# Seven tokens per row at the start, weights cast by DMA in one burst, and the inversion and the casts moved in a fused attention and feed-forward kernel

## The chip, the cores and the metric

The kernel runs on one core of one Trainium2 chip. The time is device time in microseconds (us) of the whole program. Executions of one kernel mostly agree within a few tenths of a per cent to one per cent. Each run has a state: "slow" when it is over 1.5% above the fastest run of the same kernel, at a lower granted clock. Ratios below use fast runs only: a ratio is the mean time of one kernel's fast runs over the mean of the other's fast runs of the same rounds, so it is not quite the ratio of the medians that stand beside it.

Engines: PE is TensorE, ACT is ScalarE, DVE is VectorE, POOL is GpSimd, SP is SyncE, and SPq is the DMA queue that SyncE feeds.

## The reference

```python
# q, k, v: (8 batches, 12 heads, 448 tokens, 64); cap = 30
scores = cap * tanh((q @ k.T) / sqrt(64) / cap)
attn   = softmax(scores)                  # exp, divided by its sum over the keys
x      = attn @ v                         # -> (3584 tokens, 768)
out    = maximum(x @ w1, x @ w2) @ w_out  # w1, w2: 768x1024, w_out: 1024x768
```

## The kernel before

A pair is two heads (48 pairs), a group is three pairs (16 groups). The engine streams are scheduled by hand: the order of the Python calls is the order on each engine. The feed-forward matmuls of earlier batches are dealt out as filler between the attention steps (`F(n)` issues n of them). It uses max(a, b) = relu(a - b) + b, so w1 - w2 is made once by VectorE (`subtract`), and w2 is turned by PE so that w2 times w_out can be made once too.

The first four groups have q and k (cast to bf16 in `kqf`) transposed by PE; from group 4 on one DMA transpose (`cross`) does it, into `qkT`. A group then goes this way: evict three pairs from PSUM to `u` (two buffers), gather the softmax sums (`sums`), invert them (`rec_s`), send the reciprocals to DRAM (`rec_d`) and back as a broadcast (`rec_b`), multiply `u` by them into `xT`.

```python
    def transposes(i):                      # groups 0 to 3, one pair
        g, n = divmod(i, L)
        ps = mm_psum.tile([P, 512], f32, name="mm").bitcast(bf16)
        for j in range(8):
            nc.tensor.transpose(ps[:, j * P : (j + 1) * P], kqf[g % 2][:, n, j, :], ident)
        nc.vector.tensor_copy(qkT_of(g)[:, n, :, :].rearrange("p j c -> p (j c)"), ps)

    def invert(g, n0=0, n1=G):
        ...
        nc.vector.reciprocal(t[:m, :], sums[g, n0][:m, :])
        nc.sync.dma_start(out=d[:m, :], in_=t[:m, :])             # rec_d, in DRAM
        for h in range(2):
            nc.sync.dma_start(out=rb[64 * h : 64 * h + 64, ...],  # rec_b, two DMAs
                              in_=flat[h : h + 1, :, :].to_broadcast([64, n1 - n0, S]))

    # end of moe(b): one 128x768 output tile, token 3p + j in partition p
    rows = out[b0 * S : b0 * S + NJ * P, :].rearrange("(p j) n -> p j n", j=NJ)
    nc.sync.dma_start(out=rows[:, j, :], in_=osb)

    for i in range(N):                       # one pair after another
        ...                                  # matmuls with v, evict to u, gather, filler
        if i + 1 < N:
            qk(i + 1, 3); ex(i + 1, 4, 7)
        for f, a in todo[i]:                 # loads, casts on POOL, DMA transposes
            f(*a)
        F(6)
        if i + 2 < NT * L:
            transposes(i + 2)
        F(6)
        if i == N - 1:
            invert(g, 0, G - 1)
        elif i >= G and n == 0:
            invert(g - 1)
        if i >= G and n == 1:
            normalize(g - 1)                 # six multiplies on POOL, releases u
        ...
```

Of the kernel before, what the change touches and what calls it, by code (L numbers as in the profile page):

```python
# [10 lines left out]
def kernel(  # L11
# [11 lines left out]
    nc = tc.nc  # L23
# [13 lines left out]
    L = 3  # L37
    G = 3
    Q0 = 4 * P
    NJ = 3  # L40
    scale = 1.0 / (D ** 0.5)

    ctx.enter_context(tc.manual_schedule())
# [24 lines left out]
    kf = [t[:, :, 0:4, :] for t in kqf]  # L68
    qf = [t[:, :, 4:8, :] for t in kqf]

    ident = const.tile([P, P], bf16, name="ident")
    make_identity(nc, ident)

# [14 lines left out]
    def half(b):  # L88
        return slice(0, 64) if b % 2 == 0 else slice(64, P)

    def load(g, what, n0=0, n1=L):
        b, p = divmod(g * L, NP)
        h0, h1 = 2 * (p + n0), 2 * (p + n1)
        src = {"k": k, "q": q, "v": v}[what]
        if (g, what) not in raw:
            raw[g, what] = (
                stage.tile([P, 2 * L, NJ * D], f32, name=what + "m"),
                stage.tile([P, 2 * L if what == "q" else L, D], f32, name=what + "l"),
            )
        m, l = raw[g, what]  # L100
        nc.sync.dma_start(  # L101
            out=m[:, 2 * n0 : 2 * n1, :],
            in_=src[b, h0:h1, 0 : NJ * P, :].rearrange("h (p j) d -> p h (j d)", j=NJ),
        )
        if what == "q":
            nc.sync.dma_start(
                out=l[half(b), 2 * n0 : 2 * n1, :],
                in_=src[b, h0:h1, NJ * P : S, :].rearrange("h p d -> p h d"),
            )
        else:  # L110
            for par in range(2):
                nc.sync.dma_start(  # L112
                    out=l[64 * par : 64 * par + 64, n0:n1, :],
                    in_=src[b, h0 + par : h1 : 2, NJ * P : S, :].rearrange("h p d -> p h d"),
                )

    def cast(eng, g, what, n0=0, n1=L):

        b = g * L // NP
        m, l = raw[g, what]  # L120
        if what == "v":
            for par in range(2):
                r = slice(64 * par, 64 * par + 64)
                eng.tensor_copy(  # L124
                    vp[g % 2][:, n0:n1, par, :, r],
                    m[:, 2 * n0 + par : 2 * n1 : 2, :].rearrange("p n (j d) -> p n j d", d=D),
                )
                eng.tensor_copy(vl[g % 2][r, n0:n1, r], l[r, n0:n1, :])
            return
        o = b % 2 if what == "q" else 0  # L130
        t = (kf if what == "k" else qf)[g % 2]
        eng.tensor_copy(  # L132
            t[:, n0:n1, o : o + NJ, :].rearrange("p n j (h d) -> p n h j d", h=2),
            m[:, 2 * n0 : 2 * n1, :].rearrange("p (n h) (j d) -> p n h j d", h=2, d=D),
        )
        if what == "q":
            eng.tensor_copy(
                t[half(b), n0:n1, 3 * (1 - o), :],
                l[half(b), 2 * n0 : 2 * n1, :].rearrange("p (n h) d -> p n (h d)", h=2),
            )  # L140
        else:
            for par in range(2):
                r = slice(64 * par, 64 * par + 64)
                eng.tensor_copy(t[r, n0:n1, 3, r], l[r, n0:n1, :])
# [11 lines left out]
    def load_wo(f):  # L156
        nc.gpsimd.dma_start(
            out=wo_sb[:, f : f + 2, :], in_=moe_w_out[f * P : (f + 2) * P, :].rearrange("(c p) n -> p c n", p=P)
        )
# [39 lines left out]
    def qkT_of(g):  # L199
        if g not in qkT:  # L200
            qkT[g] = stage.tile([P, L, 8, P], bf16, name="qkT")
        return qkT[g]

    def transposes(i):

        g, n = divmod(i, L)
        ps = mm_psum.tile([P, 512], f32, name="mm").bitcast(bf16)
        for j in range(8):
            nc.tensor.transpose(ps[:, j * P : (j + 1) * P], kqf[g % 2][:, n, j, :], ident)  # L209
        nc.vector.tensor_copy(qkT_of(g)[:, n, :, :].rearrange("p j c -> p (j c)"), ps)  # L210

    def cross(g):

# [4 lines left out]
    def qk(i, j):  # L218

        g, n = divmod(i, L)  # L220
        t = qkT[g][:, n, :, :].rearrange("p j c -> p (j c)")
        o = Q0 + 64 * (i // NP % 2)
        qTn = t[:, o : o + S]
        if j == 0:
            tanh[i] = att.tile([P, 7, S], bf16, name="tanh", bufs=1)
            expo[i] = att.tile([P, 7, S], bf16, name="expo")
        s = s_psum.tile([P, 2, 512], f32, name="s")
        if j < NJ:
            for h in range(2):
                r = slice(64 * h, 64 * h + 64)  # L230
                nc.tensor.matmul(s[:, h, :S], t[r, j * P : (j + 1) * P], qTn[r, :])  # L231
            nc.scalar.activation(tanh[i][:, 2 * j : 2 * j + 2, :], s[:, :, :S], AF.Tanh, scale=scale / cap)  # L232
        else:
            nc.tensor.matmul(s[:, 0, :S], t[:, 3 * P : 4 * P], qTn)  # L234
            nc.scalar.activation(tanh[i][:, 6, :], s[:, 0, :S], AF.Tanh, scale=scale / cap)  # L235

    def ex(i, c0, c1):
        nc.scalar.activation(expo[i][:, c0:c1, :], tanh[i][:, c0:c1, :], AF.Exp, scale=float(cap))  # L238
# [71 lines left out]
    def moe(b):  # L310
# [12 lines left out]
        for t in range(3) if b % 2 == 0 else range(3, 7):  # L323
            osb = opool.tile([P, DM], f32, name="osb")
            ts = slice(t * P, (t + 1) * P)
            for half in range(2):
                hs = slice(half * (DM // 2), (half + 1) * (DM // 2))
                ps = mm_psum.tile([P, 512], f32, name="mm")
                for c in range(KC):
                    nc.tensor.matmul(ps[:, : DM // 2], x[:, c, ts], wm_sb[:, c, hs], start=(c == 0), stop=False)  # L330
                    yield
                for f in range(FC):
                    nc.tensor.matmul(  # L333
                        ps[:, : DM // 2], g[:, f, ts], wo_sb[:, f, hs], start=False, stop=(f == FC - 1)
                    )
                    yield
                nc.vector.tensor_copy(osb[:, hs], ps[:, : DM // 2])  # L337
            if t == 3:
                for n in range(2):
                    r0 = (b - 1 + n) * S + NJ * P  # L340
                    nc.sync.dma_start(out=out[r0 : r0 + 64, :], in_=osb[64 * n : 64 * n + 64, :])
            else:
                b0, j = (b, t) if t < 3 else (b, t - 4)
                rows = out[b0 * S : b0 * S + NJ * P, :].rearrange("(p j) n -> p j n", j=NJ)
                nc.sync.dma_start(out=rows[:, j, :], in_=osb)

    fill_q = []

# [7 lines left out]


    NL = N // L
    NT = 4
    todo = [[] for _ in range(N)]  # L360

    def at(i, f, *a):
        todo[i].append((f, a))

    for g in range(2, NL):
        e = 0 if g < NT else 2
        at(3 * g - 6 - e, load, g, "k")
        at(3 * g - 5 - e, load, g, "q")
        at(3 * g - 4, load, g, "v")
        at(3 * g - (5 if e else 4), cast, nc.gpsimd, g, "k")  # L370
        at(3 * g - (5 if e else 3), cast, nc.gpsimd, g, "q")
        at(3 * g - 2, cast, nc.gpsimd, g, "v")
        if g >= NT:
            at(3 * g - 4, cross, g)
    at(1, cast, nc.gpsimd, 1, "v")
    at(0, load_wo, 6)
    for c in range(KC):
        at(1 + c, load_w2, c)
        at(2 + c, load_w1, c)
    MS = 3  # L380

    fill_const(nc.vector, 0)
    fill_const(nc.gpsimd, 1)
    load_wo(0)
    for n0, n1 in ((0, 1), (1, L)):
        for what in "kqv":
            load(0, what, n0, n1)
    for what in "kqv":
        load(1, what)
    for what in "kq":  # L390
        cast(nc.vector, 0, what, 0, 1)
    transposes(0)
    cast(nc.vector, 0, "v", 0, 1)
    for what in "kqv":
        cast(nc.vector, 0, what, 1, L)
    qk(0, 0)
    qk(0, 1)
    ex(0, 0, 4)
    qk(0, 2)
    qk(0, 3)  # L400
    ex(0, 4, 7)
    cast(nc.gpsimd, 1, "k")
    load_wo(2)
    cast(nc.gpsimd, 1, "q")
    load_wo(4)
    transposes(1)
    qk(1, 0)
    qk(1, 1)

    for i in range(N):  # L410
# [22 lines left out]
        if hp == 3 and b > 1:  # L433
            fill_q.append(moe(b - 1))
        F(4 if late else 8)
        if i + 1 < N:
            qk(i + 1, 3)
            ex(i + 1, 4, 7)
        for f, a in todo[i]:
            f(*a)  # L440
        F(6)
        if i + 2 < NT * L:
            transposes(i + 2)
        F(6)
        if i == N - 1:
            invert(g, 0, G - 1)
        elif i >= G and n == 0:
            invert(g - 1)
        if i >= G and n == 1:
            normalize(g - 1)  # L450
        if i + 2 < N:
            qk(i + 2, 0)
            qk(i + 2, 1)
# [7 lines left out]
    normalize(N // G - 1, G - 1, G, nc.vector)  # L461
    fill_q.append(moe(B - 1))
    F(10 ** 9)

# [1 line left out]
_INS = ['q', 'k', 'v', 'cap', 'moe_w1', 'moe_w2', 'moe_w_out']  # L466
_OUTS = [((3584, 768), 'float32')]
# [30 lines left out]
```

## Time and profile before

| | before |
|---|---|
| time, median of 3 runs | 391.78 us (391.11 to 392.51) |
| span of the profiled run | 390.3 us |
| PE busy | 358.5 us (92%), full after some 80 us |
| PE busy in the first 80 us | 57.91 us |
| end of the last normalization with a DMA transpose ahead of it (group 13) | 325.4 us |
| one group in the steady part | 20.2 us |

The busy line and the slices say which engine is full and when; the list of waits says who waits for whom; a timeline of one engine gives the order in which a queue that never overtakes works off its list. The prediction shows and reads these lines.

### The profile page before, as it was taken

The page shows a single profiled execution, that of the slowest core. Times are in us where ns is not written, and L with a number is a line of the kernel's source. Part 1 is how long each engine was busy: PE and PEld are TensorE (multiplying, and loading weights), DVE is VectorE, ACT ScalarE, POOL GpSimd, SP SyncE. Part 2 cuts the span into 40 slices and gives each one's busy share as a digit, 9 for nine tenths or more (in the row PEclk, how much of TensorE's full clock was granted, in tenths as well). Part 3 has the DMA queues.
Part 4 walks back from the last instruction along what each step waited for, and adds up shares of the span by engine and source line. Part 5 has one row for each costly group of instructions (what it writes and reads, how often), then busy time and mean ns, then how long its engine had stood idle before and what let it go on. Part 6 is the DMA issues. An engine that isn't in the chain of part 4 may idle for free.

```text
span 390.3 us, 5720 instructions
## 1 busy us (share of the span) xinstructions
PE 358.5 (92%) x2128; PEld 171.8 (44%) x2128; DVE 164.3 (42%) x248; ACT 292.4 (75%) x289; POOL 199.6 (51%) x254
## 2 busy tenths in 40 slices
PE   3468896999999999989998999999999999999995
PEld 1123443544444444434443445444444444455563
DVE  5332657774434533253325433352345333633421
ACT  2699995878899799978998899889998899400000
POOL 4272269674638374656657464729482733651000
PEclk9995998999999999999999999999999999999999
DMA  6998899786779768967989597969796751322022
GB/s 142 280 252 180 242 288 274 198 202 165 149 199 252 198 171 199 260 181 192 217 225 223 142 237 210 255 166 225 219 188 179 166 142 65 90 73 100 23 81 81
DMA packets 106596, 71.50 MB, mean 183 GB/s; under 512 B 61384, under 2 KB 99400, under 8 KB 106568
## 3 DMA queue, kind: packets, MB, share of 16 engines
q1 hardware_dynamic: 104616, 67.99, 67.6%
q0 software_dynamic: 1952, 3.15, 4.6%
q8 instruction: 16, 0.26, 0.3%
q14 instruction: 12, 0.10, 0.1%
HBM read 53.48 MB, written 11.18 MB: 166 GB/s over the span
## 4 chain that ended last, share of the span: by engine, by line
PE 54%; DMA 17%; ACT 7%; SPq 6%; POOL 6%; DVE 5%; issue 3%; POOLq 0%; DVEq 0%; ACTq 0%
PE mm L318 15%; PE mm L333 11%; PE mm L330 9%; PE pv L250 8%; DMA rec_d<-rec_s 7%; DMA rec_b<-rec_d 6%; POOL xT L305 6%; PE s L231 5%; ACT expo L238 3%; ACT tanh L232 3%; DMA vm<-in_v_dram 3%; PE pv L259 2%; SPq L112 2%; SPq L101 1%; DMA xT<-in_moe_w_dram 1%
## 5 line engine op out<-in xcount | busy, mean ns | idle before, releaser
L232 ACT ACTIVATE tanh<-s 128x896 bf16<-128x896 f32 x144 | 126.0, 909 | 36.2 <-PE s L231 35.9
L305 POOL TENSOR_TENSOR xT<-u,rec_b 64x448 bf16<-64x448 f32 x95 | 108.2, 1139 | 86.1 <-DMA rec_b<-rec_d 73.8
L238 ACT ACTIVATE expo<-tanh 128x1792 bf16<-128x1792 bf16 x96 | 144.9, 1510 | 3.0
L265 DVE COPY u<-pv 128x896 f32<-128x896 f32 x48 | 52.3, 1091 | 105.3 <-PE pv L259 80.6
L333 PE MATMUL mm<-wo_sb,gT 128*128 128x384 bf16 x448 | 88.8, 327 | 0.0
L318 PE MATMUL mm<-xT,wd_sb 128*128 128x448 bf16 x384 | 80.8, 353 | 3.3 <-POOL xT L305 1.7
L330 PE MATMUL mm<-wm_sb,xT 128*128 128x384 bf16 x336 | 68.0, 327 | 1.8 <-DVE osb L337 1.8
L250 PE MATMUL pv<-expo,vp 128*128 128x448 bf16 x288 | 66.3, 367 | 1.1 <-ACT expo L238 1.1
L333 PEld LDWEIGHTS <-gT 128*128 128x128 bf16 x448 | 41.9, 98 | 36.5 <-issue 10.8
L337 DVE COPY osb<-mm 128x384 f32<-128x384 f32 x56 | 31.0, 555 | 59.9 <-PE mm L333 54.9
L318 PEld LDWEIGHTS <-wd_sb 128*128 128x128 bf16 x384 | 35.4, 98 | 43.9 <-issue 14.5
L231 PE MATMUL s<-qkT 64*128 64x448 bf16 x288 | 46.0, 370 | 7.7 <-DVE qkT L210 5.2
L322 DVE TENSOR_SCALAR gT<-mm 128x448 bf16<-128x448 f32 x64 | 39.9, 623 | 29.6 <-PE mm L318 28.6
L330 PEld LDWEIGHTS <-xT 128*128 128x128 bf16 x336 | 31.7, 98 | 28.6 <-issue 8.7
L250 PEld LDWEIGHTS <-vp 128*128 128x128 bf16 x288 | 28.2, 101 | 29.1 <-issue 7.7
L132 POOL CAST kqf<-qm 128x1152 bf16<-128x1152 f32 x15 | 17.2, 1147 | 33.9 <-DMA qm<-in_q_dram 33.7
L235 ACT ACTIVATE tanh<-s 128x448 bf16<-128x448 f32 x48 | 26.0, 542 | 4.3 <-PE s L234 4.1
L124 POOL CAST vp<-vm 128x576 bf16<-128x576 f32 x30 | 19.9, 665 | 14.2 <-DMA vm<-in_v_dram 9.4
L132 POOL CAST kqf<-km 128x1152 bf16<-128x1152 f32 x15 | 17.2, 1147 | 12.7 <-DMA km<-in_k_dram 11.9
L231 PEld LDWEIGHTS <-qkT 64*128 64x128 bf16 x288 | 10.9, 96 | 22.8 <-issue 15.1
L209 PE MATMUL mm<-ident,kqf 128*128 128x128 bf16 x96 | 9.8, 248 | 11.5 <-DVE kqf L132 7.7
L186 PE MATMUL mm<-wo_sb,w2T 128*128 128x384 bf16 x96 | 18.7, 328 | 0.0
(44 smaller groups left out, 158.9 us busy)
## 6 DMA issues: line engine op xcount, KB each, us to landing
rec_b<-rec_d SPq DMA_DIRECT2D x30, 336.0 KB, 5.0
out_dram<-osb SPq DMA_DIRECT2D x24, 384.0 KB, 3.9
km<-in_k_dram SPq DMA_DIRECT2D x15, 576.0 KB, 7.0
qm<-in_q_dram SPq DMA_DIRECT2D x15, 576.0 KB, 4.5
vm<-in_v_dram SPq DMA_DIRECT2D x15, 576.0 KB, 4.4
xT<-in_moe_w_dram SPq DMA_DIRECT2D x6, 512.0 KB
wo_sb<-in_moe_w_out_dram POOLq DMA_DIRECT2D x4, 384.0 KB, 7.3
gT<-in_moe_w_dram POOLq DMA_DIRECT2D x6, 256.0 KB, 5.8
```

The lines of the kernel that those rows point to most:

```text
L132: eng.tensor_copy(t[:, n0:n1, o : o + NJ, :].rearrange("p n j (h d) -> p n h j d", h=2), m[:, 2 * n0 : 2 * n1, :].rearrange("p (n h) (j d) ...
L231: nc.tensor.matmul(s[:, h, :S], t[r, j * P : (j + 1) * P], qTn[r, :])
L232: nc.scalar.activation(tanh[i][:, 2 * j : 2 * j + 2, :], s[:, :, :S], AF.Tanh, scale=scale / cap)
L238: nc.scalar.activation(expo[i][:, c0:c1, :], tanh[i][:, c0:c1, :], AF.Exp, scale=float(cap))
L250: nc.tensor.matmul(ps[:, h, :S], vp[g % 2][:, n, h, j, :], e[:, 2 * j + h, :], start=(j == 0), stop=False)
L265: nc.vector.tensor_copy(U[g][:, :, n, :], pvt[i][:, :, :S])
L305: eng.tensor_mul(xT[b // 2][r, hp, cs], U[g][r, h, n, :], rec[g, n0][r, n - n0, :])
L318: nc.tensor.matmul(ps[:, :S], wd_sb[:, c, f * P : (f + 1) * P], x[:, c, cs], start=(c == 0), stop=(c == KC - 1))
L322: nc.vector.tensor_relu(g[:, f, cs], ps[:, :S])
L330: nc.tensor.matmul(ps[:, : DM // 2], x[:, c, ts], wm_sb[:, c, hs], start=(c == 0), stop=False)
L333: nc.tensor.matmul(ps[:, : DM // 2], g[:, f, ts], wo_sb[:, f, hs], start=False, stop=(f == FC - 1))
L337: nc.vector.tensor_copy(osb[:, hs], ps[:, : DM // 2])
```

## The change

Its intent: the start should need fewer and longer DMA rows, the weights should arrive early, and the normalization of a group should be done sooner, so that its buffer comes free sooner. Four parts:

1. In the first four groups a partition holds seven consecutive tokens of a head (1792-byte rows), and one DMA loads k or q where two or three did. The transposes become 26 of 64x64 and one of 128x128 per pair. The output rows of the first two batches are then ordered by seven too, and their stores are written in another form.
2. w_out and w2 are cast by DMAs that POOL issues back to back near the start. The w1 loads stay where they were.
3. The cast of v moves to the front of its iteration's list, one iteration earlier.
4. `invert` moves ahead of the list of loads and casts (`todo`), and so does `normalize`.

```diff
+            for a in range(2):                     # transposes(i), 26 of them
+                r = slice(64 * a, 64 * a + 64)
+                nc.tensor.transpose(ps[r, to : to + 64], x[r, c : c + D], ident[r, r])
+        nc.tensor.transpose(ps[:, NJ * P : Q0], x[:, NJ * P : Q0], ident)
 ...
-                rows = out[b0 * S : b0 * S + NJ * P, :].rearrange("(p j) n -> p j n", j=NJ)
-                nc.sync.dma_start(out=rows[:, j, :], in_=osb)
+                if wide:                           # batches 2 to 7: the same store as before
+                    nc.sync.dma_start(out=o[: NJ * P, :].rearrange("(p j) n -> p j n", j=NJ)[:, j, :], in_=osb)
+                else:                              # batches 0 and 1: six stores
+                    o = o.rearrange("(r j) n -> j r n", j=R7)
+                    nc.sync.dma_start(out=o[2 * j : 2 * j + 2, :, :], in_=osb)
 ...
         for g >= 4:  # iteration of each load; k, q, v
-            3g - 8, 3g - 7, 3g - 4
+            3g - 9, 3g - 8, 3g - 7
 ...
+        if i == N - 1:
+            invert(g, 0, G - 1)
+        elif i >= G and n == 0:
+            invert(g - 1)
         if i + 1 < N:
             qk(i + 1, 3)
             ex(i + 1, 4, 7)
+        if i >= G and n == 1:
+            normalize(g - 1)
         for f, a in todo[i]:
             f(*a)
         F(6)
         if i + 2 < NT * L:
             transposes(i + 2)
         F(6)
-        if i == N - 1:
-            invert(g, 0, G - 1)
-        elif i >= G and n == 0:
-            invert(g - 1)
-        if i >= G and n == 1:
-            normalize(g - 1)
```

(The load times are condensed to two lines here; the loads, the casts and the start are cut.)

More of the change, by code (lines that the diff above doesn't have):

```diff
@@ L40 @@
     NJ = 3
+    NT = 4
+    R7 = S // 64
     scale = 1.0 / (D ** 0.5)
@@ L69, with flat @@
     qf = [t[:, :, 4:8, :] for t in kqf]
+    def flat(g):
+        return kqf[g % 2].rearrange("p n j c -> p n (j c)")
     ident = const.tile([P, P], bf16, name="ident")
@@ L89, in half, with rows, raw_of @@
         return slice(0, 64) if b % 2 == 0 else slice(64, P)
+    def rows(t, b, h0, h1):
+        return t[b, h0:h1, :, :].rearrange("h (r j) d -> (h r) (j d)", j=R7)
+    def raw_of(g, what):
+        if (g, what) not in raw:
+            raw[g, what] = stage.tile([P, 2 * L * NJ * D + (2 * L if what == "q" else L) * D], f32, name=what + "r")
+        t = raw[g, what]
+        m = t[:, : 2 * L * NJ * D].rearrange("p (h c) -> p h c", c=NJ * D)
+        l = t[:, 2 * L * NJ * D :].rearrange("p (h d) -> p h d", d=D)
+        return t, m, l
     def load(g, what, n0=0, n1=L):
@@ L94, in load @@
         src = {"k": k, "q": q, "v": v}[what]
-        if (g, what) not in raw:
-            raw[g, what] = (
-                stage.tile([P, 2 * L, NJ * D], f32, name=what + "m"),
-                stage.tile([P, 2 * L if what == "q" else L, D], f32, name=what + "l"),
+        t, m, l = raw_of(g, what)
+        if g < NT and what == "v":
+            x = rows(src, b, h0, h1).rearrange("(h r) c -> r h c", r=64)
+            for a in range(2):
+                nc.sync.dma_start(
+                    out=m[64 * a : 64 * a + 64, 2 * n0 : 2 * n1, :], in_=x[:, :, NJ * D * a : NJ * D * (a + 1)]
+                )
+            for par in range(2):
+                nc.sync.dma_start(
+                    out=l[64 * par : 64 * par + 64, n0:n1, :], in_=x[:, par::2, 2 * NJ * D :]
+                )
+            return
+        if g < NT:
+            nc.sync.dma_start(
+                out=t[:, n0 * S : n1 * S].rearrange("p (n c) -> p n c", c=S),
+                in_=rows(src, b, h0, h1).rearrange("(n p) c -> p n c", p=P),
             )
-        m, l = raw[g, what]
+            return
         nc.sync.dma_start(
@@ L119, in cast @@
         b = g * L // NP
-        m, l = raw[g, what]
+        x, m, l = raw_of(g, what)
         if what == "v":
@@ L128, in cast @@
                 eng.tensor_copy(vl[g % 2][r, n0:n1, r], l[r, n0:n1, :])
+            return
+        if g < NT:
+            x = x[:, n0 * S : n1 * S].rearrange("p (n c) -> p n c", c=S)
+            if what == "q":
+                eng.tensor_copy(flat(g)[:, n0:n1, Q0 : Q0 + S], x)
+                return
+            eng.tensor_copy(flat(g)[:, n0:n1, : NJ * P], x[:, :, : NJ * P])
+            for par in range(2):
+                r = slice(64 * par, 64 * par + 64)
+                eng.tensor_copy(kf[g % 2][r, n0:n1, 3, r], x[r, :, NJ * P :])
             return
@@ L207, in transposes @@
         ps = mm_psum.tile([P, 512], f32, name="mm").bitcast(bf16)
-        for j in range(8):
-            nc.tensor.transpose(ps[:, j * P : (j + 1) * P], kqf[g % 2][:, n, j, :], ident)
-        nc.vector.tensor_copy(qkT_of(g)[:, n, :, :].rearrange("p j c -> p (j c)"), ps)
+        x = flat(g)[:, n, :]
+        todo = [(j * D, (j % 3) * P + (j // 3) * 64) for j in range(6)]
+        odd = i // NP % 2
+        todo += [(Q0 + j * D, Q0 + (64 * j if not odd else 0 if j == 6 else 64 + 64 * j)) for j in range(R7)]
+        for c, to in todo:
+            for a in range(2):
+                r = slice(64 * a, 64 * a + 64)
+                nc.tensor.transpose(ps[r, to : to + 64], x[r, c : c + D], ident[r, r])
+        nc.tensor.transpose(ps[:, NJ * P : Q0], x[:, NJ * P : Q0], ident)
+        nc.vector.tensor_copy(qkT_of(g)[:, n, :, :].rearrange("p j c -> p (j c)")[:, : Q0 + S], ps[:, : Q0 + S])
     def cross(g):
@@ L221, in qk @@
         t = qkT[g][:, n, :, :].rearrange("p j c -> p (j c)")
-        o = Q0 + 64 * (i // NP % 2)
+        o = Q0 + (64 * (i // NP % 2) if g >= NT else 0)
         qTn = t[:, o : o + S]
@@ L337, in moe @@
                 nc.vector.tensor_copy(osb[:, hs], ps[:, : DM // 2])
+            wide = b * NP >= NT * L
             if t == 3:
                 for n in range(2):
-                    r0 = (b - 1 + n) * S + NJ * P
-                    nc.sync.dma_start(out=out[r0 : r0 + 64, :], in_=osb[64 * n : 64 * n + 64, :])
-            else:
-                b0, j = (b, t) if t < 3 else (b, t - 4)
-                rows = out[b0 * S : b0 * S + NJ * P, :].rearrange("(p j) n -> p j n", j=NJ)
-                nc.sync.dma_start(out=rows[:, j, :], in_=osb)
+                    o = out[(b - 1 + n) * S : (b + n) * S, :]
+                    to = o[NJ * P : S, :] if wide else o.rearrange("(r j) n -> r j n", j=R7)[:, R7 - 1, :]
+                    nc.sync.dma_start(out=to, in_=osb[64 * n : 64 * n + 64, :])
+            else:
+                j = t if t < 3 else t - 4
+                o = out[b * S : (b + 1) * S, :]
+                if wide:
[3 more added lines that the diff above has]
+                    nc.sync.dma_start(out=o[2 * j : 2 * j + 2, :, :], in_=osb)
     fill_q = []
@@ L358 @@
     NL = N // L
-    NT = 4
     todo = [[] for _ in range(N)]
@@ L365 @@
     for g in range(2, NL):
-        e = 0 if g < NT else 2
-        at(3 * g - 6 - e, load, g, "k")
-        at(3 * g - 5 - e, load, g, "q")
-        at(3 * g - 4, load, g, "v")
-        at(3 * g - (5 if e else 4), cast, nc.gpsimd, g, "k")
-        at(3 * g - (5 if e else 3), cast, nc.gpsimd, g, "q")
-        at(3 * g - 2, cast, nc.gpsimd, g, "v")
-        if g >= NT:
+        if g < NT:
+            for what, e in (("k", 6), ("q", 6), ("v", 5)):
+                at(3 * g - e, load, g, what)
+            e = 0
+            at(3 * g - 5, cast, nc.gpsimd, g, "k")
+            at(3 * g - 4, cast, nc.gpsimd, g, "q")
+        else:
+            at(3 * g - 9, load, g, "k")
+            at(3 * g - 8, load, g, "q")
+            at(3 * g - 5, cast, nc.gpsimd, g, "k")
+            at(3 * g - 5, cast, nc.gpsimd, g, "q")
             at(3 * g - 4, cross, g)
-    at(1, cast, nc.gpsimd, 1, "v")
-    at(0, load_wo, 6)
+            at(3 * g - 7, load, g, "v")
+        todo[3 * g - 3].insert(0, (cast, (nc.gpsimd, g, "v")))
     for c in range(KC):
-        at(1 + c, load_w2, c)
         at(2 + c, load_w1, c)
@@ L382 @@
     fill_const(nc.vector, 0)
-    fill_const(nc.gpsimd, 1)
-    load_wo(0)
-    for n0, n1 in ((0, 1), (1, L)):
-        for what in "kqv":
-            load(0, what, n0, n1)
-    for what in "kqv":
-        load(1, what)
-    for what in "kq":
-        cast(nc.vector, 0, what, 0, 1)
+    load(0, "k", 0, 1)
+    load(0, "q", 0, 1)
+    load(0, "k", 1, L)
+    load(0, "q", 1, L)
+    load(0, "v", 0, 1)
+    load(1, "k")
+    load(0, "v", 1, L)
+    load(1, "q")
+    load(1, "v")
+    cast(nc.vector, 0, "k", 0, 1)
+    cast(nc.gpsimd, 0, "q", 0, 1)
+    fill_const(nc.gpsimd, 1)
     transposes(0)
-    cast(nc.vector, 0, "v", 0, 1)
-    for what in "kqv":
-        cast(nc.vector, 0, what, 1, L)
+    cast(nc.vector, 0, "k", 1, L)
+    cast(nc.vector, 0, "q", 1, L)
     qk(0, 0)
@@ L398 @@
     ex(0, 0, 4)
+    transposes(1)
     qk(0, 2)
@@ L401 @@
     ex(0, 4, 7)
+    cast(nc.vector, 0, "v")
     cast(nc.gpsimd, 1, "k")
-    load_wo(2)
     cast(nc.gpsimd, 1, "q")
-    load_wo(4)
-    transposes(1)
+    for f in range(0, FC, 2):
+        load_wo(f)
+    for c in range(KC):
+        load_w2(c)
+    cast(nc.gpsimd, 1, "v")
     qk(1, 0)
```

## The prediction

> **What bounds the kernel now.** I number the 48 head pairs i = 0..47; three pairs make a group g. I read the busy line and the 40 slices first, then the waits, then the timelines of POOL and of the DMA queue (SPq).
>
> ```profile
> PE 358.5 (92%) x2128; PEld 171.8 (44%) x2128; DVE 164.3 (42%) x248; ACT 292.4 (75%) x289; POOL 199.6 (51%) x254
> ...
> PE   3468896999999999989998999999999999999995
> ...
> PEclk9995998999999999999999999999999999999999
> ```
>
> PE is full from about slice 8 (80 us) to the end. Only the first fifth has gaps, and there the clock dips. Earlier work there can save some us; no part of the change shortens PE's work after it.
>
> Who waits for whom, in the whole run:
>
> ```profile
> DVE u L265 <- PE pv L259: 80.6, 34, 5.0
> POOL xT L305 <- DMA rec_b<-rec_d: 73.8, 31, 8.3
> ...
> DVE u L265 <- POOL xT L305: 24.7, 8, 4.5
> ```
>
> In eight of the groups VectorE could not evict a pair into `u` until POOL had normalized the group two back. That is a **ring**: evict, gather, invert, two DMAs through DRAM, normalize, buffer free. It is nearly as long as PE's work for the same pairs. Evictions run from 82.36 us (pair 9) to 337.9 us (pair 47): 255.5 / 38 = 6.72 us a pair, **20.2 us a group**. A ring once round per group that is longer than this takes over from PE. One group on the DMA queue, then POOL in about the same time:
>
> ```profile
> 263.75 0.51 SPq L101 DMA_DIRECT2D vm<-in_v_dram  x1
> 264.30 1.37 SPq L112 DMA_DIRECT2D vl<-in_v_dram  x2
> 265.79 4.22 SPq L214 DMA_TRANSPOSE qkT<-kqf  x1
> ...
> 272.07 0.37 SPq L285 DMA_DIRECT2D rec_d<-rec_s  x1
> 276.17 1.12 SPq L289 DMA_DIRECT2D rec_b<-rec_d  x2
> ```
>
> ```profile
> 271.34 1.15 POOL L132 CAST kqf<-km 128x1152 bf16<-128x1152 f32 x1
> 272.44 0.75 POOL L144 CAST kqf<-kl 64x192 bf16<-64x192 f32 x2
> 274.65 1.15 POOL L132 CAST kqf<-qm 128x1152 bf16<-128x1152 f32 x1 [1.46 <-DMA qm<-in_q_dram]
> 275.86 0.51 POOL L137 CAST kqf<-ql 64x384 bf16<-64x384 f32 x1
> 280.05 1.13 POOL L305 TENSOR_TENSOR xT<-u,rec_b 64x448 bf16<-64x448 f32 x1 [3.68 <-DMA rec_b<-rec_d]
> 281.71 5.92 POOL L305 TENSOR_TENSOR xT<-u,rec_b 64x448 bf16<-64x448 f32 x5 [0.53 <-DMA rec_b<-rec_d]
> ```
>
> Columns are start and duration. The reader is to see two orders. On POOL the k and q casts come **before** the normalization and fill time in which it would wait for rec_b anyway. On the queue the DMA transpose holds the sequencer 4.2 us, and it uses casts made a group earlier, so it waits for nothing.
>
> **What the Trainium skill says.** "DMA: Bandwidth & Descriptors", Anatomy of one DMA: a semaphore wait happens on the issuing sequencer before dispatch, not in the DMA engines. So a DMA that waits holds back everything behind it on SyncE. The trace agrees: the queue waited 56.3 us, 17 times, for rec_d to land before rec_b. "TensorE: Matmul & The Clock Gate", table at the top: POOL takes its instructions strictly in order; in the trace no cast overtakes a normalization that waits. "TensorEngine Tiling (Array Packing)": switching the tiling mode drains the array, column tiling turns fast weight loads off, and a small matmul has a floor of about 60 cycles (Key Properties; Restrictions; Instruction Overhead). No 64x64 tile is in this trace, so that cost is an estimate.
>
> **The change, part by part.**
>
> *Start.* A k or q load becomes one DMA in place of two or three (issues of 0.5 to 0.65 us each), with 1792-byte rows. Before, pair 0's first tanh began at 8.13 and pair 1's only at 17.14 us, where ScalarE's own work for a pair is 1.73+1.70+0.80+1.33+0.5 = 6.1 us: about 2.9 us lost to casts that wait for loads. I give back 2 us.
>
> *64x64 transposes.* A pair's eight 128x128 transposes took 0.61 us warm. Now 26 small ones and one large. With about 55 ns each (the page's column-load rule, 64/1.2 ns) that is 26 x 0.055 + 0.08 = 1.5 us, estimate: +0.9 us, up to +1.2 with drains. For pairs transposed while PE also has weight work (iterations 3 to 9), 7 x 1 = +7 us; in the first three ScalarE hides most of it.
>
> *w_out and w2 at once.* Ten POOL DMA issues (3.1 + 3.3 us in the groups) run back to back at 13 to 20 us in place of being spread to 64 us. The weights come early; they compete with the k, q, v loads. PE idled 3.1 us at 59 to 62 us behind VectorE, which waited 3.0 us for a w1 load. I count that bubble as saved: -3.5 us.
>
> *Sum of the early part:* -2 + 7 - 3.5 = +1.5. Pair 8 was evicted at 75.5 us; I take **77**.
>
> *Inversion, normalization and casts moved.* The reciprocal and its DMAs come earlier, which is meant to shorten the ring above. But the instruction lists of the changed kernel show another order from group 1 on: POOL has normalize(g-1), **then** the k and q casts of group g+2, then v, normalize(g), and so on. SyncE has the transpose of g+2, which waits for those casts, then the v load, **then** rec_d and rec_b of g. This makes a ring in every group: normalize(g-1), casts, transpose, rec_d(g), rec_b(g), normalize(g). In the kernel before, the casts stood ahead of the normalization, so the same ring went round once in two groups. Its length from the lines above and their like:
> - five multiplies after the second half of rec_b: 5.9 us
> - k and q casts: 1.85 + 1.7 = 3.6
> - transpose issue (12 of them, 3.73 to 4.83): 4.2
> - issue of the v load: 1.9
> - rec_d issue to rec_b issue: 4.1 here, 2.1 to 5.8 elsewhere; 3.6 chosen, since the queue is emptier
> - rec_b issue to its second half landed: 276.17 to 281.71 = 5.5; 5.4 chosen
>
> Sum **24.6 us a group against 20.2**. It covers normalize(2) to normalize(13): after that no transpose is left. So 11 turns.
>
> *When it begins.* normalize(1): rec_d about 2.3 us after pair 6 is evicted (77 - 13.6 + 2.3 = 65.7), +4 +5.6 +5.9 = 81.2; casts 84.8; transpose issued by 89; v load and rec_d 91.3; +3.7 +5.6 +5.9: normalize(2) ends at **106.5**. Pair 12 needs that buffer, and was evicted at 103.5 before. So the ring binds at once.
>
> *When it ends.* normalize(13): 106.5 + 11 x 24.6 = 377.1 us. Before, it ended at 319.43 + 5.93 = 325.4 us and released pair 45; from there to the end the program is the same in both. Difference +51.7: 391.8 + 51.7 = 443.5. I round down to **441**, since loads that compete less may shorten the DMAs further.
>
> **Rivals.**
> - *As intended: the earlier inversion frees `u` sooner.* For it: the 24.7 us of waits. PE's gaps after 80 us are only some 3.4 us, so with the start it gives at best 391.8 + 1.5 - 3.4, about 390. Against it: the order on POOL and SyncE.
> - *The early part decides.* 64x64 tiles cost more than their loads save, or the burst of weight loads starves v of group 1: 385 to 400. It needs the ring to be hidden, with some 5 us a group less than I sum; the lowest terms seen (5.9 + 3.5 + 3.8 + 1.9 + 2.1 + 5.4) still make 22.6.
> - *The ring binds, but shorter or longer:* at 22.6 us a group 421, at 25.7 (all typical loaded values, with an output store among them) 456.
>
> **Range and chances.** The second figure of the sum (11 turns) multiplies every error of a turn: 1 us is 11 us. So 422 to 457. I leave 0.08 for a ring that something I misread breaks, in which case the result is near 390: faster 0.03, same 0.05, slower 0.92.
>
> **What would show it.** Right: the largest wait of `u` is on POOL's normalization in nearly every group from pair 12; the transposes wait for POOL's cast of q; SyncE waits little for the reciprocal; PE shows idle time once per group, PE's busy share falls to some 83%; groups in the middle last 24 to 25 us; DMA share falls. The small transposes show some 1.5 us a pair. Wrong: groups of 20 us with PE full after 80 us; or rec_d issued before the transpose.

## The result

The changed kernel took **459.75 us** (458.3 to 465.79, 4 runs, the longest slow) against 392.14 us of the kernel before in the same rounds. The ratio of the fast runs is 1.169, with a 95% interval of 1.158 to 1.180. Direction and size were foreseen; the time lies 2.75 us above the range and 19 us above the point.

The page of the changed kernel: busy line, PE, granted clock, DMA.

```profile
PE 378.7 (83%) x2356; PEld 176.5 (39%) x2356; DVE 159.0 (35%) x241; ACT 293.0 (64%) x289; POOL 198.1 (43%) x252
...
PE   4778299999935969669788969979986979898996
...
PEclk9989879999996979959979997979997989999999
...
DMA  8998959674785348597485767757575707132112
```

PE, full after 80 us before, now has gaps all the way, and the clock dips after them. Its busy time rose although it does hardly more work; the mean granted clock over the run was 0.921 against 0.983. The DMA engines moved 157 GB/s on average against 183 before, so over the whole run this is not a shortage of bandwidth. From the list of waits, whole run, and from that of the DMA queue (last line):

```profile
POOL xT L354 <- DMA rec_b<-rec_d: 186.6, 29, 25.3
...
DVE u L314 <- POOL xT L354: 67.8, 11, 9.1
...
DVE rec_s L332 <- DMA sums<-u: 21.9, 4, 11.4
...
SPq L263 <- POOL vl L158: 86.8, 12, 13.4
```

The eviction into `u` waited for the normalization 67.8 us where it had waited 24.7. On SyncE the transposes waited for POOL's casts 86.8 us, 12 times (the view names a cast of v; the timelines below show that it is the cast of q that ends just before). The third line was not foreseen.

A turn is once round the ring, from the end of one group's normalization to the end of the next. One ordinary turn, on POOL and then on the queue (start, duration):

```profile
240.11 5.92 POOL L354 TENSOR_TENSOR xT<-u,rec_b 64x448 bf16<-64x448 f32 x5 [0.26 <-DMA rec_b<-rec_d]
246.09 1.14 POOL L173 CAST kqf<-kr 128x1152 bf16<-128x1152 f32 x1
...
249.19 0.51 POOL L178 CAST kqf<-qr 64x384 bf16<-64x384 f32 x1
...
264.18 1.13 POOL L354 TENSOR_TENSOR xT<-u,rec_b 64x448 bf16<-64x448 f32 x1 [12.45 <-DMA rec_b<-rec_d]
266.14 5.88 POOL L354 TENSOR_TENSOR xT<-u,rec_b 64x448 bf16<-64x448 f32 x5 [0.83 <-DMA rec_b<-rec_d]
```

```profile
249.72 3.67 SPq L263 DMA_TRANSPOSE qkT<-kqf  x1
...
256.86 0.37 SPq L334 DMA_DIRECT2D rec_d<-rec_s  x1
259.97 1.12 SPq L338 DMA_DIRECT2D rec_b<-rec_d  x2
```

This is the predicted ring: the multiplies end at 246.03, the casts at 249.70, the transpose is issued 0.02 us later, and only behind it and the load of v does rec_d go out. POOL then stands 12.45 us with no cast left to fill the time.

Two turns were long. The same queue in the first of them, where L400 is the new store of the first two batches:

```profile
125.69 2.37 SPq L400 DMA_DIRECT2D out_dram<-osb  x1
128.17 3.90 SPq L324 DMA_DIRECT2D sums<-u  x2
132.18 9.08 SPq L263 DMA_TRANSPOSE qkT<-kqf  x1
143.41 0.62 SPq L400 DMA_DIRECT2D out_dram<-osb  x1
144.13 0.53 SPq L334 DMA_DIRECT2D rec_d<-rec_s  x1
154.65 1.15 SPq L338 DMA_DIRECT2D rec_b<-rec_d  x2
```

Behind the store at 125.69 the transpose took 9.08 us in place of 3.67, and behind the one at 143.41 rec_b could be issued only 10.5 us after rec_d, where an ordinary turn needs 3.1. The DMA engines from 128 to 166 us, in 40 slices of 0.95 us:

```profile
DMA  1211129911111999893220111110059989999810
GB/s 52 72 49 46 51 77 141 67 55 55 52 52 45 284 290 173 271 348 86 38 35 39 55 52 52 52 55 11 0 91 323 209 168 273 335 258 310 206 12 0
```

Long stretches run at some 52 GB/s with one or two tenths of the 16 engines busy, while everything waits. One tenth to two tenths of 16 engines fits two engines; a store of 384 KB (393,216 bytes) at 52 GB/s lasts some 7.6 us (worked out). "DMA: Bandwidth & Descriptors" of the Trainium skill has this in the section "Why a DMA increments its semaphore by 16 and not by 1", under "How many engines (k)": a DMA is split over the largest k up to 16 that divides the slowest dimension of both access patterns that isn't 1. The store before has 128 rows on both sides, so k = 16. The new one has a DRAM side of 2 x 64 x 768: its slowest dimension is 2, so k = 2. The rate agrees.

The semaphore updates kept in the packed trace (no view of `prof` prints them) settle it. A store of the later batches, L397 at 238.04, raises its semaphore 16 times as it lands. The one at 143.41 raises it three times, at 144.46, 154.06 and 154.45. Of the 16 updates of the rec_d issued behind it at 144.13, 14 had come by 148.04; the last two came at 154.24 and 154.63, each 0.2 us after one of the store's last two. So the part of rec_d on two engines stood behind the store, and rec_b waited for it.

In the second long turn the transpose issued at 194.31, behind the store at 192.65, took 10.64 us. The last of the six stores, at 213.95, lengthened no turn (that one took 23.54 us).

**Where the 66.3 us between the two profiled spans (456.6 and 390.3) lie.** normalize(13) ends at 395.26 where it ended at 325.4: +69.9; what follows it is 61.3 us in place of 64.9: -3.6. In the changed kernel normalize(2) ends at 103.98, and 11 turns follow in 291.3 us. Nine have a mean of 24.58 us. The two long ones have 38.34 (127.83 to 166.17) and 31.76 us (190.73 to 222.49): 13.8 + 7.2 = 21 us more than the mean of the others.

The early part, in the lists of ScalarE and PE of the changed kernel:

```profile
6.79 1.73 ACT L281 ACTIVATE tanh<-s 128x896 bf16<-128x896 f32 x2 [4.76 <-PE s L280]
12.87 1.73 ACT L281 ACTIVATE tanh<-s 128x896 bf16<-128x896 f32 x2
```

```profile
21.06 0.60 PE L257 MATMUL mm<-ident,kqf 64*64 64x64 bf16 x26
21.59 0.23 PE L258 MATMUL mm<-ident,kqf 128*128 128x128 bf16 x1
```

Pair 1 began 4.3 us earlier than before (12.87 against 17.14). The order of the first loads and the place of `transposes(1)` changed too, and no run takes the seven-token rows alone, so what they are worth isn't shown. The twenty-six small transposes and the large one took 0.76 us together (21.06 to 21.82), where eight large ones took 0.61: 0.15 us more for a pair. But VectorE then waited 9.6 us at one stretch for the second block of w1, up to 54.24 us, and PE idled 9.1 us behind it, so that the lead was gone: pair 8 was evicted at 78.1 us, against 75.5 before.

### The profile page after: what moved, and what is told of

Same layout as the page of the kernel before. It is cut to its first block, busy times and chain, and to the rows that moved or that the text cites. A ratio compares the mean times of both kernels' runs of the same rounds, so it can differ in the third digit from the quotient of the medians.

```text
span 456.6 us, 6136 instructions
## 1 busy us (share of the span) xinstructions
PE 378.7 (83%) x2356; PEld 176.5 (39%) x2356; DVE 159.0 (35%) x241; ACT 293.0 (64%) x289; POOL 198.1 (43%) x252
## 4 chain that ended last, share of the span: by engine, by line
DMA 27%; POOL 23%; PE 23%; SPq 11%; issue 5%; ACT 5%; DVE 4%; POOLq 0%; DVEq 0%
POOL xT L354 16%; DMA rec_d<-rec_s 11%; DMA rec_b<-rec_d 11%; PE mm L367 8%; SPq L263 4%; PE pv L299 3%; PE mm L382 3%; POOL kqf L173 3%; PE mm L379 2%; ACT expo L287 2%; SPq L142 2%; ACT tanh L281 2%; DMA xT<-in_moe_w_dram 2%; PE mm L227 2%; DMA sums<-u 2%
## 5 line engine op out<-in xcount | busy, mean ns | idle before, releaser
L367 PE MATMUL mm<-xT,wd_sb 128*128 128x448 bf16 x384 | 88.3, 372 | 32.3 <-DVE gT L371 11.5
L382 PE MATMUL mm<-wo_sb,gT 128*128 128x384 bf16 x448 | 91.8, 335 | 0.0
L379 PE MATMUL mm<-wm_sb,xT 128*128 128x384 bf16 x336 | 71.8, 340 | 16.3 <-DVE osb L386 16.3
L299 PE MATMUL pv<-expo,vp 128*128 128x448 bf16 x288 | 68.8, 377 | 1.8 <-DVE vp L154 1.0
L367 PEld LDWEIGHTS <-wd_sb 128*128 128x128 bf16 x384 | 36.6, 101 | 76.8 <-issue 50.0
L280 PE MATMUL s<-qkT 64*128 64x448 bf16 x288 | 47.8, 382 | 6.5 <-ACT tanh L281 3.5
L386 DVE COPY osb<-mm 128x384 f32<-128x384 f32 x56 | 30.4, 545 | 55.9 <-PE mm L382 55.9
L154 POOL CAST vp<-vr 128x576 bf16<-128x576 f32 x30 | 20.9, 695 | 2.4 <-DMA vr<-in_v_dram 2.0
L257 PE MATMUL mm<-ident,kqf 64*64 64x64 bf16 x312 | 8.5, 206 | 14.3 <-DVE wm_sb L232 9.1
L283 PE MATMUL s<-qkT 128*128 128x448 bf16 x48 | 17.6, 366 | 0.7 <-ACT tanh L281 0.7
L308 PE MATMUL pv<-expo,vl 64*128 64x448 bf16 x96 | 17.9, 369 | 0.0
```

The lines of the kernel that those rows point to most:

```text
L280: nc.tensor.matmul(s[:, h, :S], t[r, j * P : (j + 1) * P], qTn[r, :])
L299: nc.tensor.matmul(ps[:, h, :S], vp[g % 2][:, n, h, j, :], e[:, 2 * j + h, :], start=(j == 0), stop=False)
L367: nc.tensor.matmul(ps[:, :S], wd_sb[:, c, f * P : (f + 1) * P], x[:, c, cs], start=(c == 0), stop=(c == KC - 1))
L379: nc.tensor.matmul(ps[:, : DM // 2], x[:, c, ts], wm_sb[:, c, hs], start=(c == 0), stop=False)
L382: nc.tensor.matmul(ps[:, : DM // 2], g[:, f, ts], wo_sb[:, f, hs], start=False, stop=(f == FC - 1))
L386: nc.vector.tensor_copy(osb[:, hs], ps[:, : DM // 2])
```

## The experiments

Each kernel ran beside the kernel before on the same chip, whose median was 392.1 to 393.4 us in the rounds. All gave the right result. The theory after the result: (T1) the order "normalize, then casts" on POOL makes the ring; (T2) the six stores with two outer rows make the two long turns. Rivals: one of the two does all of it; the early part or the DMA load matters more.

### Stores split so that both parts divide over 16 engines

```diff
-                    nc.sync.dma_start(out=o[2 * j : 2 * j + 2, :, :], in_=osb)
+                    for a in range(2):
+                        nc.sync.dma_start(out=o[2 * j + a, :, :], in_=osb[64 * a : 64 * a + 64, :])
```

> The changed kernel, with each of the six output stores of 2x64 rows written as two stores of 64 rows. My theory: the two long turns of the ring (38.3 and 31.8 us where the other nine average 24.6) come from these stores, which in that stretch ran at 52 GB/s with two tenths or less of the DMA engines busy; with them gone every turn is 24 to 26 us and the time falls by 13.8 + 7.2 = 21 us, to 437-441. Rival: the long turns come from crowding on the queue in general; then the time stays at 455-462.

Measured: 440.76 us (439.81 to 442.92), ratio 1.124. normalize(2) ends at 106.76 and normalize(13) at 377.10: 11 turns of 24.58 us, the shortest 22.6 and the longest 25.7, none long. So the stores cost 17.6 us of 66.2 in this kernel (medians of the fast runs: 458.35, 440.76, 392.14), and what remains is the ring as summed.

### Casts of k and q ahead of the normalization, stores as in the change

```diff
-        if i >= G and n == 1:
-            normalize(g - 1)
         for f, a in todo[i]:
             f(*a)
+        if i >= G and n == 1:
+            normalize(g - 1)
```

> The changed kernel, with the k and q casts put back ahead of the normalization in the third iteration of each group; narrow stores kept. My theory: the ring round each group is cut, groups fall to some 20 us where no narrow store is in the way, and the time falls by 11 x (24.6 - 20.2) = 48 us or somewhat less, to 405-420. Rival: the ring is not the cause and the narrow stores and early loads are; then it stays above 440.

Measured: 422.79 us (421.12 to 427.4), ratio 1.079, a little above what was expected. The order is worth 35.6 us here (fast runs). VectorE still waits 18.1 us for the sums, three times, behind the narrow stores.

### Both

> Both mends: wide stores, casts first. My theory: only the early part is left of the change; 390-397, as pair 8 is some 3 us late and the rest is as before or a little better. Rival: the two are not additive because the ring hides the stores; then a2 is already near 400 and a3 gains under 10 us over it.

Measured: 392.35 us (390.46 to 393.81), ratio 1.0009 with an interval of 0.995 to 1.007: the same as before. PE in its page:

```profile
PE   2786929999999999999999999999999999999995
```

PE is full again from slice 7 on, and in the steady part more so than before: from 80 to 320 us it is busy 239.15 of 240 us, against 236.64. `u` never waits for POOL in the list of waits (24.7 us before). That gain of 2.5 us is what the early inversion was meant to bring; the start takes it back, with PE busy 55.26 of the first 80 us against 57.91. The two mends together leave nothing of the regression, so no third part is needed. But the two parts overlap: the stores cost 17.6 us where the ring is the limit and 30.4 us where it isn't (422.79 - 392.35); the order costs 35.6 us beside narrow stores and 48.4 us without (440.76 - 392.35). Alone they would make 78.8 us, together they made 66.0.

### The kernel before with the changed order on POOL alone

```diff
+        # casts of v from the list of this iteration
+        if i >= G and n == 1:
+            normalize(g - 1)
+        # casts of k and q, loads, DMA transposes
```

> The kernel before, with nothing changed but the order on POOL: v cast, normalization, then k and q casts. My theory: the ring alone makes a turn of 24 to 25.5 us against 20.2, so 11 turns cost 42 to 58 us: 434-450. Rival: the order alone costs little and the harm needs the other moves: under 405.

Measured: 448.78 us (447.19 to 449.83), ratio 1.143. Its 11 turns take 275.97 us, 25.09 each. Loads, transposes, inversion and stores are those of before: the order of the two jobs on POOL makes the ring by itself.

### The kernel before with narrow stores alone, and a control

The six stores of the first two batches are each cut in two: at row 122 of 128, so that 122 and 6 rows give k = 2 and 6, and in the control at row 112, so that 112 and 16 rows give k = 16 twice. Number of DMAs and bytes are the same.

```diff
+                if b < 2:
+                    nc.sync.dma_start(out=rows[:122, j, :], in_=osb[:122, :])
+                    nc.sync.dma_start(out=rows[122:, j, :], in_=osb[122:, :])
+                else:
                     nc.sync.dma_start(out=rows[:, j, :], in_=osb)
```

> The kernel before, with the six stores of the first two batches cut at row 122 of 128: 122 is 2 x 61, so by the page such a store would run on 2 of the 16 DMA engines, like the changed kernel's. My theory: each holds two engines for some 7 us and with them every DMA behind it; 405-425, with 50 GB/s stretches. Rival: a store that few engines carry does no harm alone: within 2%.

> Control for the narrow store: the kernel before, with the six stores of the first two batches cut at row 112 of 128 (112 + 16 rows), so that there are as many stores as in the run cut at row 122 (423.6 us) but both parts divide over 16 engines. Theory (the two-engine store alone costs the 31 us): within 2% of before, 389 to 397 us. Rival (the extra store, its issue on SyncE, does it): 410 us or more.

Measured: 423.63 us (418.59 to 425.36; two of the four runs slow; ratio of the fast ones 1.0715) with the cut at 122, and, in the control run after it, 393.13 us (389.3 to 396.6, one of four slow; ratio 0.998) at 112. Six stores on two engines cost some 28 us by the fast runs (7.15% of 392; the 31 us in the expectation count the slow ones) in a kernel that has nothing else of the change; the six more DMAs cost nothing that can be seen. The queue at the same store, first cut at row 122, then at 112 (L346 and L347 are its two parts):

```profile
108.97 0.29 SPq L346 DMA_DIRECT2D out_dram<-osb  x1
109.31 1.01 SPq L347 DMA_DIRECT2D out_dram<-osb  x1
110.42 0.31 SPq L285 DMA_DIRECT2D rec_d<-rec_s  x1
119.72 1.47 SPq L289 DMA_DIRECT2D rec_b<-rec_d  x2
```

```profile
107.76 0.37 SPq L346 DMA_DIRECT2D out_dram<-osb  x1
108.18 0.42 SPq L347 DMA_DIRECT2D out_dram<-osb  x1
108.69 0.36 SPq L285 DMA_DIRECT2D rec_d<-rec_s  x1
112.29 1.13 SPq L289 DMA_DIRECT2D rec_b<-rec_d  x2
```

The issue of a narrow store is as short as that of any other, so it looks free on the queue. What it costs shows at the next DMA that somebody waits for: rec_d, 10.5 KB, landed (and so released rec_b) 9.3 us after its issue began, against 3.6. The semaphore updates show the same as before: the store raised its semaphore last at 119.11 and 119.34, and of rec_d's 16 updates 14 had come by 113.25, the last two at 119.46 and 119.70. In the control all 16 came between 111.71 and 112.27.

### The early inversion taken back (from "both")

`invert` goes back behind the PE transposes, with `normalize` behind it, as in the kernel before.

> Both mends, and the inversion put back where it stood before. My theory: w1 goes out ahead of rec_d again, so the early wait shrinks to the 3 us that it had, but some of the 3.4 us of gaps by late normalizations return: 387-391. Rival: the earlier inversion was worth much in the steady part: 393 and more.

Measured: 403.4 us (398.01 to 410.15; two of four runs slow; ratio of the fast ones 1.018, interval 1.010 to 1.027). The rival of the expectation was right. `u` waits for POOL 29.0 us again, 8 times (in the profiled run, which was a slow one, so that only the kind of the wait is read from it). The early inversion is worth some 7 us beside the other parts (ratio 1.018 against 1.0009), but this rests on two fast runs, and it is unclear.

### Where the start's gain went

Five runs, all with wide stores and casts first, ask why an earlier start gave nothing. First, the first two w1 loads one iteration (or two) earlier:

```diff
     for c in range(KC):
-        at(2 + c, load_w1, c)
+        at(2 + c if c > 1 else 1, load_w1, c)
```

> Both mends, and the first two w1 loads issued two iterations earlier, ahead of the inversion's DMAs on the queue. My theory: VectorE's 7.6 us wait for the second w1 load, which stood behind rec_d's landing and three k and q loads, is gone; 383-387, clear of the kernel before. Rival: the DMA engines are full in that stretch, so the wait moves to another load: 389-393.

Measured: 395.18 us (391.87 to 397.4), ratio 1.007 with an interval of 1.0015 to 1.0121: if anything a little slower, and above both expectations. The rival was right in kind, the wait moved: VectorE no longer waits for the second block (7.6 us in "both"), it waits 5.7 us for the third, from 56.4 to 62.1 us.

Then, on top of this, w_out and w2 spread over the first iterations as before (the burst undone):

> As the one with both mends and early w1, but w_out and w2 spread over the iterations as in the kernel before. My theory: sending them in one go is worth at most 2 us: within 2 us of it. Rival: the burst costs (it delays the k, q, v loads): faster by over 2 us; or it is what makes the start quick: slower by over 4.

Measured: 393.05 us (391.19 to 394.64), ratio 1.002. The burst is worth nothing that these runs can tell from zero.

Next, the loads of groups 4 and later put back by one or two iterations, with and without the early w1:

```diff
-            at(3 * g - 9, load, g, "k"); at(3 * g - 8, load, g, "q"); at(3 * g - 7, load, g, "v")
+            at(3 * g - 8, load, g, "k"); at(3 * g - 7, load, g, "q"); at(3 * g - 5, load, g, "v")
```

> The corrected change (wide stores, casts first, first two w1 loads early) with the loads of k, q and v for groups 4 and later put back by one to two iterations. Theory: the DMA engines are full until 60 us because the loads of the later groups moved forward too, so that the wait of VectorE for a w1 block only moved to the third block (5.7 us); with the loads later that wait shrinks below 3 us and the time is 385 to 390 us against some 392 of before. Rival: the engines are full in any order up to there, the wait goes to another load, and the time is 391 to 396 us.

> The same later loads, but the first two w1 loads where the change has them (the kernel with wide stores and casts first, 392 us). Theory: if the queue of loads is what delays w1, the second w1 block comes earlier than its 7.6 us of wait, and the time is 387 to 392 us. Rival: the second w1 load is held by its place in the issue order (behind the landing of the sums), then the wait stays at 6 to 8 us and the time at 391 to 395 us.

Measured: 390.84 us (388.35 to 397.46, one of six runs slow, ratio 0.996) with early w1, and 391.72 us (389.82 to 392.38, ratio 0.997) without. Neither interval leaves out 1. The first lies at the border of the two expectations: the w1 wait did shrink, to 0.5 us, but another took its place. VectorE in that run:

```profile
41.54 0.49 DVE L332 RECIPROCAL rec_s<-sums 48x56 f32<-48x56 f32 x1 [6.60 <-DMA sums<-u]
41.96 0.62 DVE L219 COPY w2T<-mm 128x1024 bf16<-128x1024 bf16 x1
42.51 0.63 DVE L259 COPY qkT<-mm 128x960 bf16<-128x960 bf16 x1
```

VectorE works in order too: the reciprocal of the first group, moved forward by the change, stands 6.6 us in front of the eviction of the next pair's transposes, while its sums wait among the loads. In the second run VectorE waits 7.8 us for the second w1 block, as the rival said: that load is held by its place in the issue order.

Last, these together: wide stores, casts first, early w1, late loads, weights spread, and the inversion of group 0 alone back behind the transposes.

> The best of the parts together: the run with wide stores, casts first, early w1 and late loads (390.8 us), with w_out and w2 spread as before and with the inversion of the first group alone back behind the transposes, because in that run VectorE stood 6.6 us in front of the first group's sums (34.9 to 41.5 us) with the qkT evictions behind it. Theory: that 6.6 us gap goes, PE is busier by some 4 us before 80 us, and the time is 385 to 389 us. Rival: the DMA engines are full up to 60 us whatever the order, the wait goes to another load, and the time is 389 to 394 us.

Measured: **387.46 us** (385.08 to 389.73, 6 runs), ratio 0.986 with an interval of 0.981 to 0.991: 1.4% faster than before, clear of noise.

```profile
PE   3767977999999999999999999999999999989995
```

PE is busy 59.42 us of the first 80 (before 57.91) and 239.58 of the next 240 (before 236.64). The two differences, 1.5 and 2.9 us, make up most of the 5.1 us between the medians. It still has a gap: a w1 wait of 4.5 us. This run joins two edits, so it doesn't tell what each of them is worth.

## Why the prediction was right in kind and 19 us short

**The ring: right.** It named the order on POOL and on SyncE as what would take over from PE, in every group from the third to the fourteenth, and both ways of testing it agree: the order alone turns the kernel before into one of 448.78 us, and undoing it gives 48.4 us back once the stores are wide.

**The sum of a turn: right at 24.6, partly by errors that cancel.** The eleven turns of the run with wide stores, read term by term, have these means:

| term | predicted | measured |
|---|---|---|
| five multiplies | 5.9 | 5.89 |
| casts of k and q | 3.6 | 3.64 |
| transpose issue | 4.2 | 3.71 |
| between transpose and rec_d (v load, stores) | 1.9 | 2.69 |
| rec_d issue to rec_b issue | 3.6 | 2.96 |
| rec_b issue to its second half landed | 5.4 | 5.68 |
| sum | 24.6 | 24.57 |

**Begin and end: right.** normalize(2) was put at 106.5 us and ended at 103.98 (106.76 with wide stores); normalize(13) was put at 377.1 and ended at 377.10 with wide stores. Put against the run in which only the stores are mended, the prediction of 441 us met 440.76. So close a match is partly luck: terms of the turn and of the early part cancel, and the 2.5 us that the prediction rounded down, for another reason, stand against a shorter tail. The tail is some 4 us shorter than "the same in both"; no run looked into that.

**The step that failed: the stores.** The sum of a turn has "issue of the v load: 1.9" and "rec_d issue to rec_b issue: ... 3.6 chosen, since the queue is emptier", and no term for what a store of the first two batches does to the DMAs behind it. The rewritten form of the store was read as a matter of row order. It runs on two engines; the six of them add 13.8 and 7.2 us to two turns, and the run with wide stores alone is 17.6 us faster (fast runs). The page that states the rule was among those read for the prediction (another section of it is quoted), and the diff shows the `2 * j : 2 * j + 2` in front. The rival of a longer ring, "at 25.7 (all typical loaded values, with an output store among them) 456", came near in number, for another reason: it counted the store's issue, not its two engines.

**The 64x64 transposes: mis-sized.** "26 x 0.055 + 0.08 = 1.5 us" was 0.76 us, so that the +7 us of the early part (7 x 1) was 7 x 0.15, about +1. The rule behind the 55 ns stands in "TensorE: Matmul & The Clock Gate", section "LDWEIGHTS (loading the stationary operand)", not in the tiling page. The sum takes the 26 one after another; in the trace the starts within a pair of them are 3 to 4 ns apart, and after the first pair one follows every 32 ns (first start 21.063, last 21.467 us). **The bubble behind w1: wrong in sign.** "I count that bubble as saved: -3.5 us" grew to 9.1 us of PE idle, since the second w1 load went out behind more loads and behind rec_d. **The start:** -2 us was -4.3. The errors nearly cancel (-2.3, -6 and some +9.5 us against the prediction): pair 8 was put at 77 us and was evicted at 78.1.

**The chances:** 0.92 for slower was right; the range was too narrow because it came from the spread of one sum's terms and held nothing for a term that was missing.

## What to carry to other kernels

When a change moves work on an in-order engine, write down the ring of waits that the new order closes and add up its terms: the sum against the bound engine's time per group tells whether it takes over. When a change rewrites a DMA's access pattern, look at the slowest dimension of both sides even where bytes and row order are unchanged: a store that nobody waits for can hold up the DMAs behind it, and it shows in the time when one of these is waited for. And where the DMA engines are full, a load moved forward pushes another back, so look at which wait takes the place of the one removed.

## What the Trainium skill lacked or had wrong

- "DMA: Bandwidth & Descriptors" states how many engines a DMA gets, but not what a low count costs the DMAs behind it. Here a 384 KB store on two engines ran at some 52 GB/s, a 10.5 KB DMA behind one took 9.3 us in place of 3.6, and six such stores cost 28 us of 392 (fast runs) in a kernel that differs in nothing else.
- "TensorEngine Tiling (Array Packing)" gives no time for a transpose by 64x64 tiles. The 26 of a pair and the large one behind them took 0.76 us here, against 0.61 for eight large ones. The floor of about 60 cycles a matmul (Instruction Overhead; 25 ns at 2.4 GHz, an estimate with the clock from "TensorE: Matmul & The Clock Gate", table at the top) is not contradicted: the 26 start 16 ns apart on average, but two at a time, and the pairs 32 ns apart. That fits the same page's statement that different tiles can work in parallel (Key Properties), which the prediction did not use. The large one starts 0.12 us after the last small one; whether that is the drain at the switch of tiling mode, no run shows.
- No page gives in microseconds how long SyncE's sequencer is held by a DMA transpose from SBUF to SBUF of this size (128 x 3072, bf16); "DMA: Bandwidth & Descriptors" has only a cycle count for one of 8,192 tiles, in its part on a later chip. Here it was 3.6 to 3.8 us in the changed kernel, 3.7 to 4.8 us in the kernel before, and 9.1 and 10.6 us behind a store on two engines.
